# First batch of an attention + expert kernel: packed x rows, weights loaded and converted up front, the weights' product beside the first block

## The chip, the cores and the metric

The kernel runs on one core of one Trainium2 chip. The metric is the device time of one execution in microseconds (us), as the median of several runs. All arithmetic is on the chip; the host only lays the inputs out anew.

## The reference

`x` is 4 batches of 12480 rows of 128 numbers, `inducing` is 32 rows of 128. A first attention lets the 32 inducing rows look at all rows of a batch and gives 32 pooled rows `h`; a second lets every row of `x` look at the 32 pooled rows. Each output row then goes through an expert layer of width 2048 with a rational activation.

```
def mab(q, kv):
    s = scale * (q @ kv.transpose(0, 2, 1));  s = s - s.max(-1, keepdims=True)
    a = np.exp(s);  a /= a.sum(-1, keepdims=True) + 1e-09
    return a @ kv
h = mab(I, x);  y = mab(x, h)

h = y @ w_in                                   # 128 -> 2048
P = a[0] + a[1]*h + a[2]*h**2 + a[3]*h**3
Q = 1 + |b[0]|*|h| + |b[1]|*h**2
out = (P / (Q + 1e-6)) @ w_out                 # 2048 -> 128
```

The weights `w_in` and `w_out` arrive as 64-bit floats, shown to the kernel as 64-bit integers.

## The kernel before, in words

A batch is cut into 26 blocks of 480 rows (`BT`). Groups of four blocks (seven groups, `NG`) share the attention steps. The kernel has three parts.

**Boot (`before`)** serves batch 0 alone. `pass1(0)` loads x by columns (`wide_columns`, 960 KB a group), multiplies by the inducing rows on PE, and DVE copies the scores into `e` with their maxima; ACT takes the exponentials (`exp_rows`). `pooled(0)` turns `e` on PE (`turned`, `pt`), ACT copies it to `eT`, and PE multiplies it with x by rows (`wide_rows`, three blocks to a tile) into `ph`, which DVE adds up in `acc`. A column of ones behind each x row (the 129th) gives the sum of the weights. `fold`, a reciprocal and a product give the pooled rows `HT`. All these x tiles live in the nine slots of one big tile called `row`, taken in turn. The 11 weight pieces (`raw`, five of `w_in`, six of `w_out`) are loaded in the middle of this; `convert_weights` makes 32-bit floats of each with three DVE TENSOR_SCALAR, three DVE SCALAR_TENSOR_TENSOR and one POOL addition between the last two of them. `Params` loads the six numbers a and b and `derive` works some 90 tiny DVE operations on them. In `before` the instructions are not pinned to program order; a scheduler orders them.

**Start of the main part (`main`)**: in program order from here on. Block group 0 goes through `pass3` (scores against `HT`: `pd`, `sT`, `ps`, `a`, turned back: `pa`, split into `hl`, spread by 16 small DMAs into `at`). Then two of four `piece`s fold `HT` into `w_in` (`pg`, `gs`, `st`), `shift_parts` builds `by` and `same` on POOL, and `w_out` is scaled on DVE.

**The units**: 832 units, eight for each of the 104 blocks. A unit is `first` (PE, `hp`), for every second unit a further product with `by`, `same` into `hp` (`moved`); a mask on DVE or an absolute value on ACT; a DVE product into `l`; logarithms and sigmoids of ten units at a time on ACT, over several slots of `row`; a last product on DVE and POOL; and, 17 units after `first`, `second` (PE, `po`). Engines run in order. A block's last unit also needs `lin`, made by `linear` from `w_two` and `base`; for batch 0 these come from `products` (the sum over `w_out` on DVE, 16 turns of `w_in`, 32 products `pl`). Between the units `side` lets two generators go on as a plan of spare time allows: `attend` (later groups' `pass3`) and `ahead` (first `products`, `linear(0)`, `bounded(0)`, then `pass1`, `pooled` and the pieces of the next batch). While `linear` of batch 0 is not ready, only `ahead` goes on:

```
for which in ("attend", "ahead") if not self.fast or "linear" in self.ready_cols[0] else ("ahead",):
```

PSUM tiles in boot and at the start of main come from a ring of three (`misc`, tag `hp`).

Of the kernel before, what the change touches and what calls it, by code (L numbers as in the profile page):

```python
# [9 lines left out]
F32 = mybir.dt.float32  # L10
# [25 lines left out]
def convert_weights(nc, t, raw, dst, width):  # L36

    words = raw.bitcast(I32).rearrange("p (f two) -> p f two", two=2)
    lo, hi = words[:, :, 0], words[:, :, 1]
    a, b, c = (t[:, width * i:width * i + width].bitcast(I32) for i in range(3))  # L40
# [6 lines left out]
    V.tensor_scalar(out=c, in0=hi, scalar1=0x7FF00000, scalar2=None, op0=ALU.bitwise_and)  # L47
    nc.gpsimd.tensor_tensor(out=bf, in0=bf, in1=af, op=ALU.add)
    V.scalar_tensor_tensor(out=dst, in0=c, scalar=float(0x38100000), in1=bf, op0=ALU.is_ge, op1=ALU.mult)

# [141 lines left out]
class Kernel:  # L192
# [37 lines left out]
    def misc(self, name):  # L230
        self.holder = self.who
        if self.boot:
            return self.ps_h.tile([P, 2, 512], F32, tag="hp", name=name)[:, 0]
        return self.ps_m.tile([P, 512], F32, tag="misc", name=name)

    def free(self):
        self.holder = None

    def cast(self, engine, out, in_):
# [106 lines left out]
    def wide_columns(self, b):  # L346
# [8 lines left out]

        ts = [load(g) for g in range(min(4, self.NG))]
        for g in range(self.NG):
            if g + 4 < self.NG:
                ts.append(load(g + 4))
            t = ts.pop(0)  # L360
            for j in range(4):
                yield t[:, BT * j:BT * j + BT]
                if j == 0 and g > 0:
                    self.wide_rows(b)

    def wide_rows(self, b):

        xs = self.xs.setdefault(b, [])
        n = min(3 * HB, self.NCH - HB * len(xs))
        if n > 0:  # L370
            t = self.room(f"xw{b}_{len(xs)}")[0:TP, 0:n * (C + 1)].rearrange("p (c d) -> p c d", d=C + 1)
            self.nc.sync.dma_start(out=t[:, :, 0:C], in_=self.x_t[b, :, HB * len(xs):HB * len(xs) + n, :])
            self.nc.gpsimd.memset(t[:, :, C:], 1.0)
            xs += [t[:, HB * i:HB * i + HB] for i in range(n // HB)]
# [71 lines left out]
    def pooled(self, b, own=None):  # L446
# [16 lines left out]

        eTs, early = [], int(self.boot)
        while self.e_done.get(b, 0) < self.NG:
            self.flush()
            yield "wait", 0
        if early:
            yield from turned(0)
        for g in range(self.NG):  # L470
            nb = min(4, self.NB - 4 * g)
# [5 lines left out]
            for k in range(HB * nb):  # L477
# [8 lines left out]
                nc.tensor.matmul(ph[M * c:M * c + M, 0:C + 1], eT[:, c, M * j:M * j + M], xs[4 * g + j][:, c, :], start=(j == 0), stop=(j == nb - 1))  # L486
                if c == HB - 1 and not self.boot and 4 * g + j + 4 < self.NB:
                    xs.append(self.x_rows(b, 4 * g + j + 4))
            yield "v", 0.2
            if g == 0:  # L490
                nc.vector.tensor_copy(out=acc, in_=ph[:, 0:C + 1])
            else:
                nc.vector.tensor_tensor(out=acc, in0=ph[:, 0:C + 1], in1=acc, op=ALU.add)
            self.free()
# [59 lines left out]
    def split(self, b, which, st, g):  # L554
# [10 lines left out]
        self.ready_cols[b].add(which)  # L565

    def products(self):


        nc, cp, ap, p = self.nc, self.cp, self.ap, self.params  # L570
        self.w_two = cp.tile([C, C], F32, name="w_two")
        self.base = cp.tile([P, C], F32, name="base")
        both = ap.tile([P, 512], F32, tag="gs", name="both", bufs=2)
        level, w_sum = both[:, 0:P], both[:, P:P + C]
        nc.gpsimd.tensor_scalar(out=level, in0=self.ident, scalar1=0.0, scalar2=p.lin_shift, op0=ALU.mult, op1=ALU.add)
        for i in range(2):
            yield "v", 1.2
            c = slice(C // 2 * i, C // 2 * (i + 1))
            nc.vector.tensor_reduce(out=w_sum[:, c], in_=self.w_out[:, :, c].rearrange("p f d -> p d f"), axis=mybir.AxisListType.X, op=ALU.add)
        yield "pe", 0.25  # L580
# [40 lines left out]
    def thirds(self, b, g):  # L621
# [16 lines left out]
        V.memset(lin[rest, C:], 0.0)  # L638

    def bounded(self, b):  # L640

        nc, ap, p = self.nc, self.ap, self.params
        if b == 0:
            for j in range(4):
                for i, op in ((j, ALU.max), (4 + j, ALU.min)):
                    yield "v", 0.6
                    nc.vector.tensor_reduce(out=self.w_max[:, i:i + 1], in_=self.w_in[:, 512 * j:512 * j + 512], axis=mybir.AxisListType.X, op=op)
            yield "v", 0.3
            nc.vector.scalar_tensor_tensor(out=self.w_max[:, 0:4], in0=self.w_max[:, 4:8], scalar=-1.0, in1=self.w_max[:, 0:4], op0=ALU.mult, op1=ALU.max)
            nc.vector.tensor_reduce(out=self.w_max[:, 4:5], in_=self.w_max[:, 0:4], axis=mybir.AxisListType.X, op=ALU.max)  # L650
        yield "v", 0.15
# [123 lines left out]
    def ahead(self):  # L775

        if self.fast:
            yield from self.products()
            yield from self.linear(0)
            yield from self.bounded(0)  # L780
        for b in range(1, self.B):
            self.cols[b, "a"] = self.columns(b, "a")
            yield "wait", 0
            yield "wait", 0
            yield from self.pass1(b)
            yield from self.pooled(b)
            while self.left < b - 2:
# [249 lines left out]
    def before(self):  # L1037

        nc = self.nc
        self.e, self.xs, self.HT, self.issued, self.tick = {}, {}, {}, {}, 0  # L1040
        self.boot, self.direct, self.holder, self.who = True, True, None, None
# [3 lines left out]
        loads, words = self.weights(), []  # L1045
        for n, _ in enumerate(self.pass1(0)):
            if n >= 18 and n % 3 == 1:
                words += [w for w in [next(loads, None)] if w]
        self.params = Params(self.tc.nc, self.cp, self.moe_a, self.moe_b)
        for n, _ in enumerate(self.pooled(0, self.cp.tile([C, 4 * M], F32, name="HT0"))):  # L1050
            if n % 8 == 5:
                words += [w for w in [next(loads, None)] if w]
        words += list(loads)
# [3 lines left out]
        for n, (raw, dst, width) in enumerate(words):  # L1057
            convert_weights(nc, self.room(f"cv{n}"), raw, dst, width)

# [21 lines left out]
    def main(self, fast):  # L1081
# [4 lines left out]
        self.act_q, self.jobs, self.gens, self.need = [], [], {}, {}  # L1086
        self.tick, self.ended, self.boot, self.holder, self.left = 0, 0, True, None, -1
        self.splits, self.spreads, self.scored, self.fetched, self.sent = 0, 0, -1, False, (0, 0)
        self.direct = True
# [22 lines left out]
    def again(self):  # L1112

        for n, (raw, dst, width) in enumerate(self.weights()):
            convert_weights(self.nc, self.room(f"cva{n}"), raw, dst, width)
        self.main(False)
# [58 lines left out]
```

## Time and profile before

| | |
|---|---|
| median of 3 runs | 2311.43 us (2310.86 to 2311.54) |
| the profiled execution: its time, its span | 2313.14 us, 2311.3 us |
| PE, DVE, ACT, POOL busy | 2146.0, 2147.9, 2101.0, 1483.0 us |
| first copy of an output block (`oT`), second, last | 182.97, 215.60, 2304.47 us |

Busy times are shares of an engine's instructions in the span; matmul ends are modelled. The three busiest engines lie close together, so a stage has to be looked at by itself. A wait in brackets is the idle time before an instruction and what ended it.

### The profile page before, as it was taken

Reading aid. Unit: us, or ns where it says so; the run is one execution under the profiler, and the core shown is the slowest. Engines: PE = TensorE matmul, PEld = TensorE weight load, DVE = VectorE, ACT = ScalarE, POOL = GpSimd, SP = SyncE. Lnnn points to the kernel's source line nnn. Section 1 sums busy time; section 2 is a strip of 40 time slices with the busy share of each in tenths; the row PEclk is TensorE's granted clock in tenths of the full one; section 3 lists DMA queues with packets and bytes.
Section 4 is the critical chain, followed back from the end, with each engine's and each line's share of the span. In section 5 each row is a group of like instructions: output and inputs, shape, how many; then the busy total and the mean of one; then the engine's idle time right before and its main releaser. Section 6 shows DMA issues by size and latency. Waiting matters only on the chain.

```text
span 2311.3 us, 23789 instructions
## 1 busy us (share of the span) xinstructions
PE 2146.0 (93%) x7744; PEld 975.0 (42%) x7744; DVE 2147.9 (93%) x2368; ACT 2101.0 (91%) x1193; POOL 1483.0 (64%) x1039
## 2 busy tenths in 40 slices
PE   5377999999899999998999999989999999999997
PEld 2133444444344444443444444434444444444443
DVE  2788999999999999999999999999999999999994
ACT  1086999999899999998999999989999999999995
POOL 0334666676666666766666676766677676766666
PEclk6588999999999999999999999999999999999999
DMA  9302220131123101311231031001101000000000
GB/s 242 96 1 86 83 80 21 48 81 44 47 90 91 58 25 50 74 60 46 76 93 55 18 87 43 26 16 54 52 22 50 23 18 31 18 19 20 18 17 15
DMA packets 117103, 120.89 MB, mean 52 GB/s; under 512 B 13289, under 2 KB 115561, under 8 KB 116969
## 3 DMA queue, kind: packets, MB, share of 16 engines
q1 hardware_dynamic: 116969, 119.28, 17.9%
q8 instruction: 63, 1.03, 0.2%
q14 instruction: 71, 0.58, 0.1%
HBM read 80.89 MB, written 25.56 MB: 46 GB/s over the span
## 4 chain that ended last, share of the span: by engine, by line
PE 47%; DVE 20%; ACT 16%; issue 12%; POOL 2%; DMA 2%; SPq 1%; DVEq 0%; POOLq 0%; ACTq 0%
PE po L176 31%; ACT row L176 13%; PE hp L176 12%; DVE l L176 10%; DVE row L176 6%; ACT L176 2%; SPq L176 1%; PE ph L176 1%; DMA row<-x_c 1%; POOL l L176 1%; PE pd L176 1%; PE pc L176 1%; POOL row L176 1%; DVE gl L176 1%; DVE oT L176 1%
## 5 line engine op out<-in xcount | busy, mean ns | idle before, releaser
L176 PE MATMUL po<-l,w_out 128*128 128x480 f32 x3328 | 1563.5, 575 | 6.1 <-POOL l L176 3.4
L176 DVE SCALAR_TENSOR_TENSOR l<-row,all,hp 128x960 f32<-128x960 f32 x832 | 999.5, 1202 | 32.4 <-ACT row L176 23.7
L176 POOL TENSOR_TENSOR l<-row 128x960 f32<-128x960 f32 x416 | 929.2, 2234 | 34.7
L176 POOL TENSOR_SCALAR row<-l,all 128x960 f32<-128x960 f32 x416 | 448.1, 1077 | 673.8 <-DVE l L176 603.8
L176 PEld LDWEIGHTS po<-l,w_out 128*128 128x128 f32 x3328 | 619.4, 191 | 405.8 <-issue 239.6
L176 ACT ACTIVATE row<-row,all 128x3840 f32<-128x3840 f32 (+1 forms) x250 | 738.1, 2953 | 1.0
L176 ACT ACTIVATE row<-row 128x3840 f32<-128x3840 f32 (+1 forms) x250 | 715.9, 2864 | 8.0 <-DVE l L176 6.8
L176 DVE SCALAR_TENSOR_TENSOR l<-l,all,row 128x960 f32<-128x960 f32 x416 | 533.3, 1283 | 4.6 <-ACT row L176 4.6
L176 PE MATMUL hp<-at,st 128*128 128x480 f16 x1664 | 477.2, 369 | 42.8 <-DVE l L176 32.9
L176 ACT ACTIVATE row<-hp,all 128x960 f32<-128x960 f32 x416 | 436.7, 1050 | 62.2 <-PE hp L176 61.3
L176 DVE TENSOR_SCALAR row<-hp 128x960 int32<-128x960 int32 x416 | 475.4, 1143 | 11.4 <-PE hp L176 10.7
L176 PEld LDWEIGHTS <-st 128*128 128x128 f16 x1872 | 181.9, 98 | 527.0 <-issue 506.8
L176 PE MATMUL hp<-same,by 96*128 96x480 f16 x832 | 239.6, 369 | 31.2 <-DVE row L176 24.6
L176 ACT ACT_TABLE_LOAD x169 | 216.8, 1283 | 3.5 <-PEq L1168 0.7
L176 PEld LDWEIGHTS <-by 96*128 96x128 f16 x832 | 82.0, 99 | 222.5 <-issue 195.6
L176 DVE COPY oT<-po 128x480 f32<-128x480 f32 x104 | 67.6, 650 | 46.5 <-PE po L176 45.6
L176 PE MATMUL po<-at,st 128*128 128x480 f16 x208 | 60.0, 370 | 3.2 <-DVE st L176 3.2
L176 ACT ACTIVATE a<-a 120x512 f32<-120x512 f32 (+2 forms) x21 | 14.7, 723 | 37.0 <-DVE a L176 37.0
L176 ACT ACTIVATE e<-e,nmc 128x960 f32<-128x960 f32 (+1 forms) x16 | 15.5, 984 | 31.5 <-DVE nmc L176 31.5
L176 DVE TENSOR_SCALAR_CACHE_REDUCE e<-pc 128x240 f32<-128x240 f32 (+1 forms) x56 | 20.6, 397 | 24.4 <-PE pc L176 24.4
L176 POOL TENSOR_TENSOR a<-a,asm 120x512 f32<-120x512 f32 (+1 forms) x27 | 38.7, 1433 | 1.7 <-PE bound L176 1.7
L176 POOL TENSOR_TENSOR row<-row 128x384 f32<-128x384 f32 (+2 forms) x11 | 11.9, 1085 | 42.8 <-DVE row L176 35.3
(117 smaller groups left out, 595.4 us busy)
## 6 DMA issues: line engine op xcount, KB each, us to landing
xTb<-x_c SPq DMA_DIRECT2D x104, 240.0 KB, 3.2
out<-oT SPq DMA_DIRECT2D x104, 240.0 KB, 2.0
xTa<-x_c SPq DMA_DIRECT2D x78, 240.0 KB, 3.3
x<-x_t SPq DMA_DIRECT2D x78, 240.0 KB, 4.0
at<-hl SPq DMA_DIRECT2D x416, 30.0 KB, 1.8
row<-x_t SPq DMA_DIRECT2D x8, 720.0 KB, 14.1
row<-x_c SPq DMA_DIRECT2D x5, 960.0 KB, 11.7
raw<-w_in SPq DMA_DIRECT2D x4, 480.0 KB, 12.0
```

The costliest lines, as they stand in the source:

```text
L176: ins = call(*args, **kw)
```

## The change

Seven edits, all in what is done for batch 0 or around its first blocks.

1. x rows for batch 0 are stored without the column of ones (slots of 128 instead of 129 floats); the sums of the weights come from DVE reductions over `e`, `n` is 128 in boot.
2. The parameters are loaded and derived first, `shift_parts` follows them; both stood later. `before` is now in program order.
3. The five `w_in` pieces are asked for ahead of x; all seven column loads are issued at once; a `w_out` piece is asked for before each row load from the third on.
4. `converted` emits the conversions between the steps of `pass1` (five) and `pooled` (six), the last operation of one behind the front of the next, in tiles of their own. Masked words overwrite `lo`.
5. `sums`: `w_out` is scaled on POOL (it was DVE), `base`'s level made, and `w_out` summed on DVE in two halves, inside `pooled`.
6. In `main` the two pieces and `products` are stepped between the steps of `pass3` of group 0, instead of behind it and among the units.
7. The maxima of `w_in` and `bounded(0)` go behind `pass1(1)`.

```
     def wide_rows(self, b):
...
+            if len(xs) >= 2 * 3:
+                self.words += [w for w in [next(self.loads, None)] if w]
-            t = self.room(f"xw{b}_{len(xs)}")[0:TP, 0:n * (C + 1)].rearrange("p (c d) -> p c d", d=C + 1)
-            self.nc.sync.dma_start(out=t[:, :, 0:C], in_=self.x_t[b, :, HB * len(xs):HB * len(xs) + n, :])
-            self.nc.gpsimd.memset(t[:, :, C:], 1.0)
+            t = self.room(f"xw{b}_{len(xs)}")[0:TP, 0:n * C].rearrange("p (c d) -> p c d", d=C)
+            self.nc.sync.dma_start(out=t, in_=self.x_t[b, :, HB * len(xs):HB * len(xs) + n, :])

+    def converted(self, words):
+        last = ()
+        for n, (raw, dst, width) in enumerate(words):
+            t = self.mp.tile([P, 2, width], I32, tag="l", name=f"cv{n}", bufs=self.rooms["l"])
+            gen = convert_weights(self.nc, t, raw, dst, width)
+            next(gen)
+            for _ in last:
+                pass
+            last = gen
+            yield
...
     def pooled(self, b, own=None):
...
+            full, rest = self.NB // 4, self.NB % 4
+            nc.vector.tensor_reduce(out=acc[:, C:], in_=e[:, 0:full].rearrange("p g n -> p (g n)"), ...)
...
+    def sums(self):
...
+        nc.gpsimd.tensor_scalar(out=self.w_out, in0=self.w_out, scalar1=p.z_rho, scalar2=None, op0=ALU.mult)
+        nc.gpsimd.tensor_scalar(out=self.base, in0=self.ident, scalar1=0.0, scalar2=p.lin_shift, ...)
+        for i in range(2):
+            yield
+            c = slice(C // 2 * i, C // 2 * (i + 1))
+            nc.vector.tensor_reduce(out=self.w_two[:, c], in_=self.w_out[:, :, c].rearrange("p f d -> p d f"), ...)
...
     def before(self):
...
+        nc.state["pin"] = True
+        self.params = Params(self.tc.nc, self.cp, self.moe_a, self.moe_b)
         self.setup()
+        self.loads, self.words = self.weights(), []
+        first = [next(self.loads) for _ in range(-(-self.F // BT))]
+        ahead = self.pass1(0)
+        next(ahead)
         self.params.derive()
+        self.shift_parts()
...
+        more = self.converted(first)
+        next(more)
+        next(more)
+        for n, _ in enumerate(ahead):
+            if n % 4 == 3:
+                next(more, None)
+        self.drive(more)
+        more = self.later_words()
+        for n, _ in enumerate(self.pooled(0, ...)):
+            if n > 8 and n % 3:
+                next(more, None)
+        self.drive(more)
+
+    def later_words(self):
+        yield from self.converted(self.words)
+        yield from self.sums()
...
     def main(self, fast):
...
-        self.drive(self.pass3(0, [range(1)]))
-        for piece in pieces[:2]:
-            self.drive(piece)
+        fill = pieces[:2] + ([self.products()] if fast else [])
+        while_held = 0
+        for _ in self.pass3(0, [range(1)]):
+            held, while_held = self.held, while_held + 1 if self.held else 0
+            while fill and while_held < 3:
+                if next(fill[0], self) is self:
+                    fill.pop(0)
+                if self.held == held:
+                    break
+        for gen in fill:
+            self.drive(gen)
         self.later = pieces[2:]
-        if fast:
-            self.shift_parts()
-            nc.vector.tensor_scalar(out=self.w_out, in0=self.w_out, scalar1=p.z_rho, scalar2=None, op0=ALU.mult)
```

`self.held` counts the PSUM tiles that `misc` has given and `free` has not had back. `next(fill[0])` is called until that count is what it was.

## Rows read from the trace of the kernel before

**Rows 1.** Busy time of each engine by stage, then clock, DMA share, GB/s.

```profile
core 0: us, PE busy (x) PEld busy (x) DVE busy (x) ACT busy (x) POOL busy (x), PEclk, DMA share, GB/s
0.00:37.70 37.70, 17.11 (x67) 3.95 (x70) 6.94 (x38) 5.51 (x7) 1.56 (x15) 0.71 1.00 255
...
70.00:94.50 24.50, 5.31 (x10) 1.22 (x10) 22.29 (x53) 0.00 (x0) 9.51 (x9) 0.57 0.27 83
94.50:106.20 11.70, 5.53 (x13) 2.60 (x14) 5.69 (x9) 4.06 (x8) 1.15 (x1) 0.57 0.05 13
106.20:131.40 25.20, 13.43 (x38) 5.27 (x39) 17.29 (x16) 8.00 (x11) 9.21 (x20) 0.73 0.05 14
131.40:215.60 84.20, 62.83 (x213) 29.55 (x213) 65.83 (x83) 66.31 (x41) 30.97 (x21) 0.84 0.13 41
338.25:2304.50 1966.25, 1904.19 (x6743) 868.04 (x6742) 1889.73 (x1909) 1896.61 (x1059) 1347.49 (x916) 0.99 0.15 44
```

**Rows 2.** Timeline of batch 0's chain, from the exponentials to the first unit.

```profile
33.47 3.65 ACT L176 ACTIVATE e<-e,nmc 128x960 f32<-128x960 f32 x4 [31.45 <-DVE nmc L176]
...
70.93 0.29 DVE L176 COPY HT<-HT 128x128 f32<-128x128 f32 x1 [0.24 <-PE HT L176]
...
94.49 0.66 DVE L176 COPY sT<-pd 128x480 f32<-128x480 f32 x1 [0.44 <-DVE w_out L176]
...
100.42 1.06 PE L176 MATMUL pa<-ident,a 120*128 120x120 f32 x4 [4.11 <-DVE a L176]
...
106.18 0.98 PE L176 MATMUL hp<-at,st 128*128 128x480 f16 x4 [1.35 <-POOL st L176]
```

**Rows 3.** Timeline of the first units: waits for `by`, the sum, `linear`.

```profile
112.94 0.98 PE L176 MATMUL hp<-same,by 96*128 96x480 f16 x2 [5.77 <-POOL by L176]
...
118.77 3.70 DVE L176 TENSOR_REDUCE both<-w_out 128x64 f32<-128x1024 f32 x2
...
180.32 1.06 PE L176 MATMUL po<-at,st 128*128 128x480 f16 x2 [3.19 <-DVE st L176]
```

**Rows 4.** ACT from 106 to 216 us: a wait, and a group of instructions.

```profile
ACT row L176 <- PE hp L176: 11.2, 2, 8.5
...
L176 ACT ACTIVATE wt<-pgt,all 128x512 f32<-128x512 f32 x4 | 2.7, 686 | 0.0
```

**Rows 5.** Windows of the load stream: columns of x, rows of x, `derive`.

```profile
8.00:17.00 9.00, 6.06 (x28) 0.74 (x28) 2.99 (x17) 0.00 (x0) 0.48 (x4) 0.94 1.01 423
20.00:30.00 10.00, 3.25 (x12) 0.45 (x12) 1.11 (x8) 0.00 (x0) 0.12 (x1) 0.50 1.11 186
56.00:66.00 10.00, 1.85 (x32) 1.09 (x24) 9.51 (x96) 0.59 (x2) 1.19 (x1) 0.50 1.02 224
```

**Rows 6.** DMA of the first 75 us: packets by size; an issue's time to landing.

```profile
DMA packets 17779, 18.01 MB, mean 240 GB/s; under 512 B 948, under 2 KB 16368, under 8 KB 17776
...
ind<-ind_c SPq DMA_DIRECT2D x1, 16.0 KB, 1.6
```

**Rows 7.** Timeline of two conversions of `w_out` pieces, from 81 us.

```profile
81.43 0.35 DVE L176 TENSOR_SCALAR row<-raw 128x384 int32<-128x384 int32 x1
...
82.64 1.15 DVE L176 TENSOR_SCALAR row<-raw 128x384 int32<-128x384 int32 x1
83.70 0.55 DVE L176 SCALAR_TENSOR_TENSOR w_out<-row 128x384 f32<-128x384 int32 x1
...
86.72 0.55 DVE L176 SCALAR_TENSOR_TENSOR w_out<-row 128x384 f32<-128x384 int32 x1
```

**Rows 8.** The page's costliest groups: a POOL TENSOR_SCALAR.

```profile
L176 POOL TENSOR_SCALAR row<-l,all 128x960 f32<-128x960 f32 x416 | 448.1, 1077 | 673.8 <-DVE l L176 603.8
```

**Rows 9.** PE's four turns and two chains of products, at either clock.

```profile
126.58 1.06 PE L176 MATMUL pgt<-ident,w_in 128*128 128x128 f32 x4
...
131.94 1.05 PE L176 MATMUL pl<-w_out,wt 128*128 128x128 f32 x8
...
142.35 2.08 PE L176 MATMUL pl<-w_out,wt 128*128 128x128 f32 x8 [0.46 <-ACT wt L176]
```

**Rows 10.** Instructions on tile `w_max`, durations min, median, max in ns.

```profile
L176 DVE TENSOR_REDUCE w_max<-w_in x8: 669/674/677, 183.5 to 201.6; 128x1 f32<-128x512 f32 x8
```

More of the change, by code (lines that the diff above doesn't have):

```diff
@@ L39, in convert_weights @@
     lo, hi = words[:, :, 0], words[:, :, 1]
-    a, b, c = (t[:, width * i:width * i + width].bitcast(I32) for i in range(3))
+    a, b = t[:, 0], t[:, 1]
     V = nc.vector
@@ L231, in misc @@
         self.holder = self.who
+        self.held += 1
         if self.boot:
@@ L237, in free @@
         self.holder = None
+        self.held -= 1
     def cast(self, engine, out, in_):
@@ L317, in weights @@
             yield raw, dst, width
+    def converted(self, words):
[8 more added lines that the diff above has]
+            yield
+        for _ in last:
+            pass
+        yield
     def x_rows(self, b, n):
@@ L354, in load @@
             return t
[L356 to L360, printed above, removed]
+        ts = [load(g) for g in range(self.NG)]
+        for g, t in enumerate(ts):
             for j in range(4):
@@ L462, in turned @@
             eTs.append(eT)
-        eTs, early = [], int(self.boot)
+        eTs, early, n = [], int(self.boot), C if self.boot else C + 1
         while self.e_done.get(b, 0) < self.NG:
@@ L469, in pooled @@
             yield from turned(0)
+            full, rest = self.NB // 4, self.NB % 4
+            nc.vector.tensor_reduce(out=acc[:, C:], in_=e[:, 0:full].rearrange("p g n -> p (g n)"), axis=mybir.AxisListType.X, op=ALU.add)
+            if rest:
+                more, rows = ap.tile([P, 1], F32, tag="mx", name=f"sum{b}"), slice(0, M * rest)
+                nc.vector.tensor_reduce(out=more[rows], in_=e[rows, full], axis=mybir.AxisListType.X, op=ALU.add)
+                nc.vector.tensor_tensor(out=acc[rows, C:], in0=acc[rows, C:], in1=more[rows], op=ALU.add)
         for g in range(self.NG):
@@ L485, in pooled @@
                     self.wide_rows(b)
[L486 removed]
+                nc.tensor.matmul(ph[M * c:M * c + M, 0:n], eT[:, c, M * j:M * j + M], xs[4 * g + j][:, c, :], start=(j == 0), stop=(j == nb - 1))
                 if c == HB - 1 and not self.boot and 4 * g + j + 4 < self.NB:
@@ L490, in pooled @@
             if g == 0:
-                nc.vector.tensor_copy(out=acc, in_=ph[:, 0:C + 1])
+                nc.vector.tensor_copy(out=acc[:, 0:n], in_=ph[:, 0:n])
             else:
-                nc.vector.tensor_tensor(out=acc, in0=ph[:, 0:C + 1], in1=acc, op=ALU.add)
+                nc.vector.tensor_tensor(out=acc[:, 0:n], in0=ph[:, 0:n], in1=acc[:, 0:n], op=ALU.add)
             self.free()
@@ L565, in split @@
         self.ready_cols[b].add(which)
-    def products(self):
[L570 to L579, printed above, removed]
+    def sums(self):
+        nc, p = self.nc, self.params
+        self.w_two = self.cp.tile([C, C], F32, name="w_two")
+        self.base = self.cp.tile([P, C], F32, name="base")
+        nc.gpsimd.tensor_scalar(out=self.w_out, in0=self.w_out, scalar1=p.z_rho, scalar2=None, op0=ALU.mult)
+        nc.gpsimd.tensor_scalar(out=self.base, in0=self.ident, scalar1=0.0, scalar2=p.lin_shift, op0=ALU.mult, op1=ALU.add)
+        for i in range(2):
+            yield
+            c = slice(C // 2 * i, C // 2 * (i + 1))
+            nc.vector.tensor_reduce(out=self.w_two[:, c], in_=self.w_out[:, :, c].rearrange("p f d -> p d f"), axis=mybir.AxisListType.X, op=ALU.add)
+    def products(self):
+        nc, ap, p = self.nc, self.ap, self.params
+        level, w_sum = self.base, self.w_two
         yield "pe", 0.25
@@ L638, in thirds, with magnitudes @@
         V.memset(lin[rest, C:], 0.0)
+    def magnitudes(self):
+        nc = self.nc
+        for j in range(4):
+            for i, op in ((j, ALU.max), (4 + j, ALU.min)):
+                yield "v", 0.6
+                nc.vector.tensor_reduce(out=self.w_max[:, i:i + 1], in_=self.w_in[:, 512 * j:512 * j + 512], axis=mybir.AxisListType.X, op=op)
+        yield "v", 0.3
+        nc.vector.scalar_tensor_tensor(out=self.w_max[:, 0:4], in0=self.w_max[:, 4:8], scalar=-1.0, in1=self.w_max[:, 0:4], op0=ALU.mult, op1=ALU.max)
+        nc.vector.tensor_reduce(out=self.w_max[:, 4:5], in_=self.w_max[:, 0:4], axis=mybir.AxisListType.X, op=ALU.max)
     def bounded(self, b):
         nc, ap, p = self.nc, self.ap, self.params
[L643 to L650, printed above, removed]
         yield "v", 0.15
@@ L785, in ahead @@
             yield from self.pass1(b)
+            if self.fast and b == 1:
+                yield from self.magnitudes()
+                yield from self.bounded(0)
             yield from self.pooled(b)
@@ L1087, in main @@
         self.tick, self.ended, self.boot, self.holder, self.left = 0, 0, True, None, -1
+        self.held = 0
         self.splits, self.spreads, self.scored, self.fetched, self.sent = 0, 0, -1, False, (0, 0)
@@ L1112, in again @@
     def again(self):
-        for n, (raw, dst, width) in enumerate(self.weights()):
-            convert_weights(self.nc, self.room(f"cva{n}"), raw, dst, width)
+        self.drive(self.converted(self.weights()))
         self.main(False)
```

20 lines of the change are left out of this document (4 added, 16 removed).

## The prediction

> **What bounds the kernel now.** I read the busy time by stage first. From 338 us to the end, ACT is busy 1897, PE 1904 and DVE 1890 of 1966 us [rows 1]: nothing in the change touches these units, and a gain must come from before. The early stages look otherwise. Up to 37.7 us DVE works 6.9 us; from 70 to 94.5 us it works 22.3 of 24.5 while ACT does nothing; from 131.4 to 215.6 us, where the units already run and logarithms and sigmoids are on, ACT is busy only 66.3 of 84.2 us [rows 1].
>
> The timeline then says what is late. `HT` of batch 0 is ready at 71.2, but the copy `sT` that uses it starts at 94.49: DVE, in order, converts weights in between [rows 2]. From `sT` the chain runs through `pa` at 100.42 to the first unit's product at 106.18 [rows 2]. That unit waits 5.8 us for POOL's `by`; DVE sums `w_out` for 3.7 us at 118.8 with the units' work behind it; and block 0's last product waits for `linear` until 180.3, since `products` had to squeeze between the units [rows 3]. ACT's 17.9 us of idleness after 131.4 hold 11.2 us in two waits for PE's `hp`, which stands behind that product [rows 4]; the rest is group 1, which `attend` may start only once `linear` is there.
>
> The load stream: with column loads alone 423 GB/s, while the row loads dominate 186 [rows 5]. The packet counts say why: 16368 of 17779 packets are under 2 KB, and the rows of x (6.39 MB in pieces of 512 bytes, 12480 of them) are most of these [rows 6]. A tile of 129 floats a row cannot take two rows in one run, one of 128 can.
>
> **The change part by part.**
>
> *Loads.* 2.1 MB of `w_in`, 6.4 of columns, 6.4 of rows and 2.1 of `w_out` are 17 MB. At 423 for the whole [rows 5], less a bit for the 1 KB runs of `w_out`, they take some 42 to 45 us after a start at 3 us: the last at 47 or so. If the rows stay at 186, they alone take 34 us instead of 15 and the last comes at about 65. I take the fast end: the columns' runs are the nearest to the new ones. `w_in` in front moves the columns by 5 us (2.1 MB at 423), but the rows no longer sit between them, so the last group lands at about 24 us.
>
> The Trainium skill, "DMA: Bandwidth & Descriptors", Specifications, puts the least transfer for line rate at 512 B, which the rows of x already are. By that sentence packing them would bring the stream nothing; the windows, 186 against 423 GB/s, speak against it [rows 5]. By it the sum below would end near 2287 instead of 2282.
>
> *DVE to the exponentials.* The parameters land first, some 3 us after issue (a lone small load took 1.6 [rows 6]), so `derive` starts near 4 and takes about 7 (its window holds 9.5 us with a piece of a conversion in it [rows 5]). Five conversions follow among the score copies. One `w_out` conversion took 3.0 us, from 83.70 to 86.72, of which 0.8 is a TENSOR_SCALAR of 1.15 us that takes 0.35 when POOL is not adding [rows 7]. Four at 3.0 and a small one at 1.2 are 13.2; 2 more for the first addition, which queues behind `shift_parts` on POOL; 6.9 for everything DVE did in this stage before [rows 1]; 2 for the trips to PE in the chain of maxima. 4 + 7 + 13.2 + 2 + 6.9 + 2 = 35 us for the start of the exponentials (33.47 before [rows 2]): the conversions are hidden in what was DVE's wait for columns. If that cover fails, each costs its 3 us.
>
> *DVE to `sT`.* Exponentials 3.7 us [rows 2], to 38.7. The new sum over `e`, 3360 elements: at 0.674 us for 512 [rows 10], 4.4, to 43. Six `w_out` conversions, 5 x 3.0 + 1.2 = 16.2, to 59.3; they stand in front of the second group's `acc`, so PE waits, its ring of three PSUM tiles full. POOL's scaling of `w_out`, 2048 columns at 1.077 us for 960 [rows 8], 2.3 us, during which DVE has nothing: 61.6. The two sums, 3.7 [rows 3]: 65.3. The groups held back need about 6, the fold and `HT` 3.4, and `pd` 2: `sT` at 76.7, **17.8 us earlier**. Bounds: 68 with conversions at 2.2 and no such waits, 88 if the words land late and nothing overlaps. The eight POOL memsets and DVE's scaling vanish, but hid behind waits: nothing.
>
> *`sT` to the first unit.* It was 11.7 us [rows 2]. Now two pieces, the base and four rounds of turns, copy and products stand in PE's queue ahead of `pa`. A round is 1.06 + 0.69 + 2.08 at the low clock and about 0.6 + 0.69 + 1.05 at the high one [rows 4, 9], plus hand-overs: 4.0 or 2.5 us, and the rounds don't overlap, as each `pl` waits for ACT's copy with the next turns behind it. The granted clock here was 0.57 [rows 1], so I lean to the low: 15 us, in place of the 4.1 that PE waited for DVE anyway. The `pg` in front of `ps` add 2. What the later pieces and `st` cost after `pa` was hidden by the small DMAs and saves nothing. I take **12 us more** (bounds 8 and 16): the first unit at 106.2 - 17.8 + 12 = 100.4, **5.8 us earlier**.
>
> *First units to 131.4.* The wait for `by` (5.8) and the sum on DVE (3.7) are gone [rows 3], the turns and `base` on PE as well (about 1): **10 us** (bounds 6 and 12).
>
> *131.4 to 215.6.* ACT loses four copies, 2.7 us [rows 4], and has 17.9 us of idle time to lose [rows 1]: 20.6 at most. `linear` is ready in the first ticks, `attend` and `ahead` start some 20 units earlier. But their DVE work then falls on the filling units; I take **16 us** (bounds 8 and 20.6).
>
> *Moved back.* The eight maxima of `w_in`, 8 x 0.67 = 5.4 us [rows 10], go from here to the preparation of batch 1, where DVE is 96% busy: **3 us lost** (bounds 0 and 5.4). The slots of `row` start at another number, which shifts the pattern of joined logarithms; it runs through all nine positions either way: nothing, at most a microsecond or two at the end.
>
> Sum: 5.8 + 10 + 16 - 3 = 28.8 us. The profiled execution took 2313.1 with a span of 2311.3; the median is 2311.4, so the same gain from it gives 2282.6, and I say **2282**. Ends with all bounds together: best 8.7 earlier at `sT` more and 4 less on the way, 2 + 4.6 + 3, or 51 us of gain (2260); worst -11.3, -4, -4, -8, -2.4, or 1 us of loss.
>
> **The rivals.**
>
> *The boot gives nothing.* DVE's order makes the start no earlier: the first unit comes at about 106, because the chain with `products` in it costs 16 and `sT` comes only at 84 to 85. For it: DVE idles during the maxima's trips, the exponentials and POOL's scaling, and in order nothing fills that. Then only the later 23 us remain: about 2288 to 2293.
>
> *The rows stay slow.* Packing changes no rate: behind the columns at 24, seven row tiles at 186 GB/s take 27 us and the `w_out` pieces among them 5 or more, so the last word lands near 58 and its conversion ends near 64 instead of 59: 5 us, 2287. The page of the Trainium skill named above would have it so; the two windows are the evidence against.
>
> *Given back.* The later units don't keep the lead: earlier work of `attend` and `ahead` lands on a full DVE, and the known stalls at the batches' ends take it, 10 to 20 us: 2292 to 2302. For it: three engines within 1% of each other [rows 1]. Against: ACT's idle time in this stage is real, and work done early isn't done twice.
>
> *All of it and more.* High clock, rounds at 2.5 us, ACT full: 2262.
>
> *Slower.* One mechanism: the last `w_out` conversions stand in DVE's queue ahead of the sums that `HT` needs, and their loads now stand behind row loads, which wait in SP's queue for slots that PE must have read. If that stream crawls, `HT` and all behind it wait. The gain behind the first unit is 23 us, so it decides when the first unit comes after 129, which by the steps above is a last word at about 47 + 29 = 76 us, 17 MB at about 230 GB/s. At 186 throughout, the last word lands at 94: about 2329. Rows 5 show 423 for long runs, so this is unlikely.
>
> **How the numbers follow.** Forecast 0.55 (2270 to 2288 is its own range), boot gives nothing 0.14, rows slow 0.08, given back 0.09, more 0.07, slower 0.05, no change 0.02. Range: 2264 to 2302 leaves out about half of "more", the slow end, and the edges of the costs not seen. Under 0.2% (4.6 us) a measurement of this kernel tells nothing. Faster by more: 0.91; within: 0.04, of which 0.02 is the end of "given back"; slower: 0.05.
>
> **What would show it.** Row loads above 350 GB/s and the last load before 50 us; exponentials at 33 to 37 us; `sT` near 77 with the `w_out` conversions ahead of `acc`; `pa` some 18 us behind `sT`, with PE's `pl` and ACT's `wt` in turn between; the first unit near 100; no wait for `by`; the first output copy 30 us earlier than 183; ACT idle under 5 us from the first logarithms to the second output copy. The prediction fails if `sT` comes after 88, if the rounds cost over 4 us each, or if the lead at the second output copy shrinks by the end by more than 10 us.

## The result, and the profile after

The changed kernel takes 2289.83 us (median of 4 runs, 2288.05 to 2293.07); the kernel before, run beside it, 2311.48 (2310.86 to 2311.94). The ratio is 0.9908, 95% interval 0.9891 to 0.9925: 21.65 us faster, 7.8 us above the forecast of 2282. That is within the range 2264 to 2302, but just outside the forecast's own 2270 to 2288 and inside the 2288 to 2293 of the rival "the boot gives nothing". The profiled execution took 2290.83 us with a span of 2288.9.

Four marks cut the gain of the profiled execution into stages: `sT`, the first unit's product, the second output copy, the last one. All numbers are us.

| stage | before | after | gain | forecast |
|---|---|---|---|---|
| to `sT` | 94.49 | 82.93 | 11.6 | 17.8 |
| `sT` to the first unit | 11.69 | 21.84 | -10.1 | -12 |
| first unit to second copy | 109.42 | 85.95 | 23.5 | 26 |
| second copy to last | 2088.87 | 2091.39 | -2.5 | -3 |
| sum | | | 22.4 | 28.8 |

Nearly all of the gain lies in the third row; the gain up to `sT` is spent again on the way to the first unit. These are lines of the timeline after (start, duration, engine, line, instruction; in brackets the wait and its releaser):

```profile
36.62 3.65 ACT L177 ACTIVATE e<-e,nmc 128x960 f32<-128x960 f32 x4 [30.55 <-DVE nmc L177]
...
39.73 3.15 DVE L177 TENSOR_REDUCE acc<-e 128x1 f32<-128x2880 f32 x1 [3.14 <-ACT e L177]
...
45.78 1.15 DVE L177 TENSOR_SCALAR cv<-raw 128x384 int32<-128x384 int32 x1
...
50.30 0.34 DVE L177 TENSOR_SCALAR cv<-raw 128x384 int32<-128x384 int32 x1
50.68 0.56 DVE L177 SCALAR_TENSOR_TENSOR cv<-raw,cv 128x384 int32<-128x384 int32 x1
51.27 0.36 DVE L177 TENSOR_SCALAR cv<-cv 128x384 int32<-128x384 int32 x1
...
58.86 0.36 DVE L177 TENSOR_SCALAR cv<-raw 128x384 int32<-128x384 int32 x1 [1.46 <-DMA raw<-w_out]
...
60.95 1.10 POOL L177 TENSOR_TENSOR cv<-cv 128x384 f32<-128x384 f32 x1 [3.96 <-DVE cv L177]
...
61.11 1.35 DVE L177 SCALAR_TENSOR_TENSOR w_out<-raw,cv 128x384 f32<-128x384 int32 x1
...
62.64 0.23 DVE L177 TENSOR_SCALAR cv<-raw 128x128 int32<-128x128 int32 x1 [0.18 <-DMA raw<-w_out]
...
65.08 5.46 POOL L177 TENSOR_SCALAR w_out<-w_out,all 128x2048 f32<-128x2048 f32 x1 [0.72 <-DVE w_out L177]
...
70.57 3.64 DVE L177 TENSOR_REDUCE w_two<-w_out 128x64 f32<-128x1024 f32 x2 [5.40 <-POOL w_out L177]
...
82.93 0.66 DVE L177 COPY sT<-pd 128x480 f32<-128x480 f32 x1 [2.04 <-PE pd L177]
...
90.06 2.08 PE L177 MATMUL pl<-w_out,wt 128*128 128x128 f32 x8 [0.84 <-ACT wt L177]
...
93.83 1.16 PE L177 MATMUL pl<-w_out,wt 128*128 128x128 f32 x8 [0.84 <-ACT wt L177]
...
99.69 0.58 PE L177 MATMUL pa<-ident,a 120*128 120x120 f32 x4
...
104.77 1.76 PE L177 MATMUL hp<-at,st 128*128 128x480 f16 x4 [4.51 <-DMA at<-hl]
106.98 0.96 PE L177 MATMUL hp<-same,by 96*128 96x480 f16 x2 [0.45 <-DVE row L177]
...
169.18 0.66 DVE L177 COPY oT<-po 128x480 f32<-128x480 f32 x1 [0.56 <-PE po L177]
...
190.72 0.66 DVE L177 COPY oT<-po 128x480 f32<-128x480 f32 x1
...
2282.11 0.66 DVE L177 COPY oT<-po 128x480 f32<-128x480 f32 x1 [11.13 <-PE po L177]
```

`sT`, `pa` and `hp` answer to [rows 2]. No conversion stands between `HT` and `sT` any more; the conversions now stand ahead of `HT`, and POOL's scaling of `w_out` makes DVE wait 5.40 us. The `pl` and `wt` of the product stand between `sT` and `pa`, and `hp` waits 4.51 us for the small DMAs. The wait for `by` of [rows 3] is gone.

The windows (busy time of PE, PEld, DVE, ACT, POOL, clock, DMA share, GB/s) answer to [rows 1] and [rows 5]:

```profile
18.00:26.00 8.00, 4.40 (x24) 0.46 (x16) 7.79 (x20) 0.00 (x0) 1.98 (x2) 0.51 1.03 383
26.00:31.00 5.00, 2.01 (x12) 0.44 (x10) 4.83 (x14) 0.00 (x0) 1.42 (x1) 0.50 1.01 225
...
46.00:51.00 5.00, 1.87 (x39) 1.22 (x36) 4.83 (x9) 0.60 (x1) 1.88 (x2) 1.00 0.99 212
51.00:56.00 5.00, 1.18 (x25) 0.64 (x24) 4.76 (x10) 0.60 (x1) 1.35 (x2) 0.63 1.03 215
...
120.00:190.72 70.72, 60.26 (x210) 23.21 (x210) 65.39 (x78) 64.57 (x37) 30.96 (x20) 0.85 0.30 90
```

In the first four, DVE works nearly all the time, where it had been mostly idle (1.11 of 10 us from 20 to 30 us in [rows 5]). The row loads, from 26 us on, run at 212 to 225 GB/s, not at the columns' rate. In the last, ACT is busy 64.57 of 70.72 us.

### The profile page after: what moved, and what is told of

Read it like the earlier page. It is cut to its first block, busy times and chain, and to the rows that moved or that the text cites. A ratio compares the mean times of both kernels' runs of the same rounds, so it can differ in the third digit from the quotient of the medians.

```text
span 2288.9 us, 23773 instructions
## 1 busy us (share of the span) xinstructions
PE 2141.9 (94%) x7744; PEld 969.5 (42%) x7744; DVE 2154.6 (94%) x2370; ACT 2101.7 (92%) x1193; POOL 1489.4 (65%) x1031
## 3 DMA queue, kind: packets, MB, share of 16 engines
q8 instruction: 63, 1.03, 0.2%
## 4 chain that ended last, share of the span: by engine, by line
PE 41%; DVE 27%; issue 14%; ACT 12%; DMA 3%; POOL 1%; SPq 1%; DVEq 0%; ACTq 0%; POOLq 0%
PE po L177 26%; DVE l L177 15%; PE hp L177 10%; ACT row L177 10%; DVE row L177 7%; DMA raw<-w_out 2%; ACT L177 1%; SPq L177 1%; PE ph L177 1%; PE pd L177 1%; DVE oT L177 1%; PE pc L177 1%; POOL l L177 1%; PE pg L177 1%; DVE asm L177 1%
## 5 line engine op out<-in xcount | busy, mean ns | idle before, releaser
L177 ACT ACTIVATE eT<-pt 120x512 f32<-120x512 f32 (+1 forms) x28 | 15.5, 558 | 31.6 <-PE pt L177 31.6
L177 POOL TENSOR_TENSOR cv<-cv 128x384 f32<-128x384 f32 (+2 forms) x11 | 12.3, 1119 | 37.3 <-DVE cv L177 37.2
L177 PE MATMUL pt<-ident,e 128*120 128x128 f32 (+1 forms) x112 | 18.3, 293 | 17.8 <-DVE acc L177 16.4
## 6 DMA issues: line engine op xcount, KB each, us to landing
row<-x_t SPq DMA_DIRECT2D x8, 720.0 KB, 21.8
row<-x_c SPq DMA_DIRECT2D x5, 960.0 KB, 11.6
```

Of the source, the lines that this page charges most:

```text
L177: ins = call(*args, **kw)
```

## The experiments

Ratios are to the kernel before, run beside each experiment (medians 2311.97 to 2312.36). Times of single instructions come from one profiled execution each, and these differ: ahead of `sT` numbers 4, 6, 7 and 12 leave the changed kernel as it is, yet their `sT` comes at 79.96, 83.10, 81.42 and 81.63 us (82.93 in the changed kernel). DVE's waits for weight words there add up to anything from 0 (number 4) to 2.84 us (number 6), and PE's steps behind them ran at either clock (granted 0.50 from 80 to 84 us in the changed kernel, 1.00 in numbers 7 and 12). So a shift of 3 us or less at `sT` shows little unless the wait or the instruction that makes it is seen too.

**1. Rows of x over 128 partitions.** The tiles of the changed kernel cover 120; here the DMA brings eight rows more, which nobody reads.

```
-            t = ...[0:TP, 0:n * C].rearrange("p (c d) -> p c d", d=C)
-            self.nc.sync.dma_start(out=t, in_=self.x_t[b, :, HB * len(xs):HB * len(xs) + n, :])
+            t = ...[:, 0:n * C].rearrange("p (c d) -> p c d", d=C)
+            flat = self.x_t.rearrange("b p n c -> (b p) n c")[TP * b:TP * b + P]
+            self.nc.sync.dma_start(out=t, in_=flat[:, HB * len(xs):HB * len(xs) + n, :])
+            t = t[0:TP]
```

> The changed kernel with its nine row loads over 128 partitions (eight rows of the next batch more, never read) instead of 120. Theory A: the rows' rate is set by the 120 partitions, not by the length of their runs; then the row stretch moves at 380 GB/s or more where the changed kernel shows 212 to 225, and the last weight piece lands near 47 us instead of 62. DVE is full with conversions from 43 to 65 us there and waits only 1.6 us for loads, so the first unit comes only 2 to 4 us earlier and the time is 2286 to 2289. Theory B: what holds the rate is the stream itself (row loads and weight loads mixed, or many loads in flight): 215 GB/s stays and so does the time, 2290.

2291.42 us (2289.26 to 2296.16), ratio 0.9914 [0.9894, 0.9935]. The windows of this kernel:

```profile
26.00:31.00 5.00, 2.02 (x12) 0.45 (x10) 4.80 (x14) 0.00 (x0) 1.41 (x1) 0.50 1.03 401
...
36.00:41.00 5.00, 2.54 (x10) 2.05 (x10) 1.20 (x2) 4.15 (x6) 0.00 (x0) 0.50 1.03 390
...
46.00:51.00 5.00, 1.41 (x35) 1.14 (x36) 4.83 (x10) 0.49 (x1) 2.12 (x2) 1.00 0.75 290
51.00:56.00 5.00, 2.26 (x35) 1.47 (x33) 4.77 (x9) 0.60 (x1) 1.17 (x1) 0.52 0.01 3
```

With 128 partitions the same rows come at about 400 GB/s and the stream ends near 50 us, as the forecast had it. In both kernels the 16 DMA engines are busy all the time on average (share 1.01 to 1.03 from 26 to 31 us), so the packets themselves take longer. Between 27 and 46 us a 6 KB packet of the rows took 446 ns (median of the trace's DMA records) with 120 partitions and 239 with 128; a 1 KB packet of `w_out`, whose loads cover 128 partitions in both, 78 and 46 ns. The slow rows thus slow their neighbours too. Yet `sT` moves by 1.6 us only (81.35), the first unit by 1.4 (103.40), where 2 to 4 were expected, and the time not measurably: DVE was full with conversions, and only its waits for words, 1.64 us, are gone.

**2. Rows not packed.** Slots of 129 floats again, the rest as changed.

```
-            t = ...[0:TP, 0:n * C].rearrange("p (c d) -> p c d", d=C)
+            t = ...[0:TP, 0:n * (C + 1)].rearrange("p (c d) -> p c d", d=C + 1)[:, :, 0:C]
```

> The changed kernel with the row slots 129 floats apart again (512-byte runs), and nothing else; the column of ones is not written and not read. Theory A (partitions): the row stretch loses at most a tenth of its rate, 190 to 205 GB/s, last weight piece 3 to 5 us later, time 2290 to 2294. The prediction's reading (run length sets the rate) would have the two alike only if packing brought nothing; if packing matters at all beyond a tenth, the time rises by over 5 us, to 2295 or more.

2294.6 us (2292.19 to 2297.77), 0.9923 [0.9905, 0.994]. Its windows:

```profile
26.00:31.00 5.00, 2.01 (x12) 0.44 (x10) 4.81 (x14) 0.00 (x0) 1.42 (x1) 0.50 1.15 187
...
46.00:51.00 5.00, 2.02 (x38) 1.52 (x37) 4.83 (x9) 0.60 (x1) 2.02 (x2) 0.84 1.14 193
```

`sT` (86.40) and the first unit (108.46) come 3.5 and 3.7 us later. In the six windows from 26 to 56 us the rate is 175 to 197 GB/s; packing is worth 19 to 40 GB/s, window by window, about a seventh. The time's interval overlaps that of the changed kernel, so what packing is worth in time is not shown.

**3. `w_out` scaled on DVE again.** (`nc.gpsimd.tensor_scalar` becomes `nc.vector.tensor_scalar` in `sums`.)

> The changed kernel with w_out scaled by DVE, at the same place, instead of by POOL. POOL's instruction took 5.46 us with DVE idle for 5.4 of them; on DVE it took 1.28 us in the kernel before. If a gain in the boot is handed on whole to the end, the copy sT comes 4.2 us earlier, at 78.7, and the time is 2285 to 2286. Rival: the units' filling or the load on DVE takes it back: 2289 or more.

2286.23 us (2283.71 to 2290.06), 0.9889 [0.9869, 0.9909]. Its timeline:

```profile
65.37 1.29 DVE L177 TENSOR_SCALAR w_out<-w_out,all 128x2048 f32<-128x2048 f32 x1
66.77 3.73 DVE L177 TENSOR_REDUCE w_two<-w_out 128x64 f32<-128x1024 f32 x2
...
78.07 0.66 DVE L177 COPY sT<-pd 128x480 f32<-128x480 f32 x1 [1.56 <-PE pd L177]
```

From the end of the last conversion to the sums DVE takes 1.4 us, not 5.6. `sT` comes 4.9 us earlier than after the change, the first unit 6.7 earlier (98.08). The medians differ by 3.6 us, less than their intervals can tell apart.

**4. The product of the weights among the units**, as before; all else as changed.

```
-        fill = pieces[:2] + ([self.products()] if fast else [])
+        fill = pieces[:2]
...
     def ahead(self):
...
+            yield from self.products()
             yield from self.linear(0)
```

> The changed kernel with products (the base, four rounds) back where it was: first thing that ahead does among the units; the pieces stay stepped into the block's chain. Theory: the gain behind the first unit comes from linear being ready in the first ticks. Then the first unit comes 8 to 9 us earlier (pa no longer behind the rounds), near 96, but the wait for linear in block 0 and the late start of attend are back (10 and 12 us in the kernel before): second output copy near 200 to 205 instead of 190.7, time 2298 to 2303. Rival: the rounds fit into the idle time of the filling units and only the earlier first unit counts: 2281 to 2284.

2302.3 us (2300.93 to 2303.63), 0.9958 [0.9946, 0.997]. Its timeline:

```profile
93.64 1.76 PE L177 MATMUL hp<-at,st 128*128 128x480 f16 x4 [4.51 <-DMA at<-hl]
...
159.38 0.65 DVE L177 COPY oT<-po 128x480 f32<-128x480 f32 x1
...
201.87 0.66 DVE L177 COPY oT<-po 128x480 f32<-128x480 f32 x1 [0.95 <-PE po L177]
```

The first unit comes 11.1 us earlier than after the change (3.0 of them already at `sT`, where nothing was changed, so the rounds cost some 8) and the first copy 9.8, but the second copy 11.2 us later, the last 10.1; the median is 12.5 us higher. An early `linear`, which sets `attend` free, is worth more than an early first unit.

**5. In the kernel before, `shift_parts` alone moved early** (behind `derive`).

> The kernel before with one part of the change alone: shift_parts (by and same on POOL) right behind derive instead of behind the first pieces. Theory: the 5.8 us that the first unit waited for by are taken off the path one for one, since all units stand behind that wait: 2305 to 2307 where the kernel before has 2311 to 2312. Rival: the wait for linear 70 us later is set by products, not by the first unit, and takes it back: 2310 to 2312.

2306.36 us (2303.32 to 2307.53), 0.9975 [0.9965, 0.9985]. Its timeline:

```profile
107.93 1.78 PE L176 MATMUL hp<-at,st 128*128 128x480 f16 x4 [1.27 <-POOL st L176]
110.16 0.96 PE L176 MATMUL hp<-same,by 96*128 96x480 f16 x2 [0.45 <-DVE row L176]
```

The 5.77 us of [rows 3] become 0.45; the first unit starts 1.7 us later, the second copy 3.7 earlier, the last 5.8 earlier, and the median falls by 6.0. Within the noise, this wait was worth its full length.

**6. Maxima and `bounded(0)` early again**, right behind `linear(0)`.

```
             yield from self.linear(0)
+            yield from self.magnitudes()
+            yield from self.bounded(0)
...
             yield from self.pass1(b)
-            if self.fast and b == 1:
-                yield from self.magnitudes()
-                yield from self.bounded(0)
```

> The changed kernel with the maxima of w_in and bounded(0) back behind linear(0), so 5.4 us of DVE among the filling units instead of in the preparation of batch 1. The prediction's step (moving them back costs 3 us) would have it up to 3 us faster, 2285 to 2289. Rival: DVE is the fuller engine among the filling units too, and the maxima cost their 5 us there: 2293 to 2296.

2279.13 us (2277.73 to 2280.18), 0.9854 [0.984, 0.9869]: 10.7 us under the changed kernel, where at most 3 were expected. First the timeline of the changed kernel, then that of this one: `HT` of batch 1 and, for this one, the second and the last copy.

```profile
565.71 0.28 DVE L177 COPY HT<-HT 128x128 f32<-128x128 f32 x1
```

```profile
191.79 0.66 DVE L177 COPY oT<-po 128x480 f32<-128x480 f32 x1
...
508.03 0.27 DVE L177 COPY HT<-HT 128x128 f32<-128x128 f32 x1
...
2271.20 0.66 DVE L177 COPY oT<-po 128x480 f32<-128x480 f32 x1 [11.12 <-PE po L177]
```

The second copy is 1.07 us later than in the changed kernel, the rest 12.0 us shorter (2079.41 for 2091.39). In the changed kernel the maxima run from 270.7 to 381.4 us; `pass1(1)`, 70 us earlier than before (maximum of its scores at 270.65, was 341.06), hands its lead to them, and `HT` of batch 1 comes at 565.71, where it was 560.76 before. With the maxima early it comes 58 us sooner.

Most of the 12.0 us lies in one stretch: the 41st to the 46th output copy take 113.5 us after the change and 103.1 here. Number 4 has 103.1 in it too, with the maxima where the change put them; its `HT` of batch 1 came at 522.60 and that of batch 2 at 972.18. These are `HT` of batch 2 in the changed kernel, in this one, and in number 12:

```profile
1021.61 0.27 DVE L177 COPY HT<-HT 128x128 f32<-128x128 f32 x1
...
956.23 0.27 DVE L177 COPY HT<-HT 128x128 f32<-128x128 f32 x1
...
1027.79 0.27 DVE L177 COPY HT<-HT 128x128 f32<-128x128 f32 x1
```

In number 12 `HT` of batch 1 comes earlier still (490.54), but that of batch 2 late, and the stretch takes 110.1 us. So in these runs the stretch is short where batch 2 is prepared early, not where batch 1 is. Number 4 has nothing of it at the end, as it was 7.7 us behind by the 41st copy, counted from the second. Why the early preparation shortens the stretch is not shown.

**7. The fill stops after 13 steps of `pass3`**, so that `pa` does not stand behind all rounds (`while fill and while_held < 3 and k < 13`).

> The changed kernel with only two of the four rounds of products stepped in ahead of pa; the other two stand behind the block's small DMAs. If the rounds are what delays pa (2.4 to 3.5 us each), pa comes at 94 to 95 instead of 99.7 and the first unit's product at 99.5 to 100.5 instead of 104.8, since the two late rounds fit into the 4.5 us that PE waited for the DMA; time 2285 to 2286. Rival: the late rounds end behind the landing and hold the first unit, which gains under 2 us: 2288 to 2290.

2288.73 us (2286.08 to 2292.47), 0.9906 [0.9889, 0.9923]: no change that can be told. `pa` starts at 91.59 (8.1 us earlier, 1.5 of them already at `sT`) and the first unit no longer waits for the small DMAs, but comes at 99.49 only; the second copy is 5.5 us earlier, the last 4.8 in the profiled execution, which was the fastest of the four.

**8. Edits 1, 3 and 7 together, and two `w_out` conversions ahead of the sum over `e`** (`if n < 2 or n > 8 and n % 3`).

> The changed kernel with row loads over 128 partitions, w_out scaled on DVE, two of the four rounds of products behind the block's DMAs, and the first two w_out conversions issued before the sum over e, where DVE waited 3.1 us for the exponentials. Theory: the steps add up in front of the first unit (1.4, 5, 5 and 3 us): sT at 73 to 76, first unit at 90 to 93, time 2277 to 2281. Rival: with the words there in time the filling units become the bound and hand on half: 2283 to 2286.

2280.52 us (2278.56 to 2282.82), 0.9865 [0.985, 0.9881]. `sT` at 75.27, first unit 92.28, second copy 177.78, last 2269.89. The lead over the changed kernel is 12.9 us at the second copy and 12.2 at the end.

**9. Edits 8 and 6 together.**

> The four edits of the run before that joined them (rows over 128 partitions, w_out scaled on DVE, two rounds of products behind the block's DMAs, two conversions ahead of the sum), and also the maxima and bounded(0) back behind linear(0). Theory: the first is worth 9 us ahead of the first unit and the second 10 us at the batches' preparation, at different places, so they add: 2268 to 2272. Rival: both move the preparation of the later batches in time and the second gain belongs to one position only: 2276 to 2281.

2265.15 us (2264.72 to 2269.17, five runs), 0.9803 [0.979, 0.9816]. Its timeline:

```profile
155.67 0.66 DVE L177 COPY oT<-po 128x480 f32<-128x480 f32 x1
...
177.21 0.66 DVE L177 COPY oT<-po 128x480 f32<-128x480 f32 x1
...
493.46 0.27 DVE L177 COPY HT<-HT 128x128 f32<-128x128 f32 x1
...
2255.95 0.66 DVE L177 COPY oT<-po 128x480 f32<-128x480 f32 x1 [11.13 <-PE po L177]
```

This beats both kernels, the changed one by 24.7 us. The two edits do not get in each other's way: number 8 by itself gave 9.3 us, number 6 gave 10.7. Together they gave 4.7 more than that sum, and 3 more than expected; where this comes from is not shown.

**10. POOL's scaling with a second operation** (`scalar2=0.0, op1=ALU.add`, which adds zero).

> The changed kernel with POOL's scaling of w_out written as multiply by the scalar and add 0 (two operations) instead of multiply alone. If the form is what made 2048 columns take 5.46 us where a two-operation instruction of this kernel takes 1.07 us for 960, it takes 2.3 us. Rival: something else about the place or the operand (16 x 128, in place): 5.4 us again.

One run, 2286.55 us. All instructions on `w_out`, POOL's line (duration in ns, least, median, most; first and last start):

```profile
L177 POOL TENSOR_SCALAR w_out<-w_out,all x1: 1972/1972/1972, 64.9 to 64.9; 128x2048 f32<-128x2048 f32 x1
```

1.97 us in place of 5.46. DVE waits 1.91 us for it, not 5.40. `sT` comes at 79.39 and the first unit at 101.01, 3.5 and 3.8 us earlier.

**11. Each row load in two DMAs, of 112 and of 8 partitions.**

```
-            self.nc.sync.dma_start(out=t, in_=self.x_t[b, :, HB * len(xs):HB * len(xs) + n, :])
+            for r in (slice(0, 112), slice(112, TP)):
+                self.nc.sync.dma_start(out=t[r], in_=self.x_t[b, r, HB * len(xs):HB * len(xs) + n, :])
```

> The changed kernel with each row load cut in two: partitions 0 to 111 and 112 to 119. If what slows the rows is that 120 partitions are no multiple of 16, the large part moves at the rate of the columns and the stretch at 330 GB/s or more. Rival: only all 128 (or a multiple of 32 or 64) reach it: 230 GB/s or less again.

One run, 2291.35 us. Its windows:

```profile
26.00:31.00 5.00, 2.01 (x12) 0.44 (x10) 4.83 (x14) 0.00 (x0) 1.42 (x1) 0.50 1.02 225
...
46.00:51.00 5.00, 3.19 (x38) 2.08 (x36) 4.79 (x10) 0.60 (x1) 1.57 (x2) 0.50 1.06 224
```

217 to 225 GB/s from 26 to 56 us, as with 120 partitions in one DMA.

**12. Maxima and `bounded(0)` later still**, behind `linear(1)`.

> The changed kernel with the maxima and bounded(0) moved further back: behind linear(1), when batch 1 is prepared, instead of between pass1(1) and pooled(1). The same work in the same batch. Theory: what they cost is that ahead stands still for them from 270 to 384 us, so that HT of batch 1 comes at 566 instead of 508 us; then HT(1) comes near 500 to 515 here, the stretch to block 35 is 4 to 6 us faster than in the changed kernel, and the end 2281 to 2287, as batch 2 is delayed instead. Rival: it is the 5.4 us of DVE in the preparation, wherever: 2289 to 2292.

2283.3 us (2279.4 to 2285.66), 0.9879 [0.9864, 0.9894], 6.5 us under the changed kernel. From second copy to last 2084.36 us: 7.0 less than after the change, 5.0 more than in number 6. `HT` of batch 1 comes at 490.54. So more than half of the price hung on the place ahead of that `HT`, and the rest is still paid in the later place. `HT` came earlier than the 500 to 515 expected and earlier than in number 6, so its time alone does not set the price.

This profiled execution shows one thing more. Nothing is changed ahead of the units, yet the timeline has the product's rounds at another clock:

```profile
86.93 1.16 PE L177 MATMUL pl<-w_out,wt 128*128 128x128 f32 x8 [0.84 <-ACT wt L177]
89.36 1.16 PE L177 MATMUL pl<-w_out,wt 128*128 128x128 f32 x8 [0.84 <-ACT wt L177]
...
100.31 1.76 PE L177 MATMUL hp<-at,st 128*128 128x480 f16 x4 [4.51 <-DMA at<-hl]
```

The first `pl` takes 1.16 us, not 2.08, and the first unit stands 18.7 us behind `sT` (81.63) in place of 21.8. From 80 to 84 us the granted clock was 1.00 here (2.4 GHz) and 0.50 after the change (1.2 GHz). In the 4 us ahead of that PE had been busy 2.70 us in both, and the clock was 0.68 on average here, 0.50 there. Why one execution got it earlier is not shown.

## Why the prediction came out as it did

**The mechanism was right behind the first unit, and the boot's was not.** The larger part of the forecast gain came as forecast: no wait for `by`, no sum over `w_out` among the units, `linear` early (`gl` of batch 0 at 113.91, was 176.13). First unit to second copy gave 23.5 us for 26; the ACT time left idle there from 120 us on is 6.2 us, a little over the 5 that were named. Numbers 4 and 5 show the two parts by themselves: 12.5 us for the product's place (net of the 8 us that the rounds cost ahead of the first unit), 6.0 for `by`. One sign failed: the first output copy came 13.8 us earlier, not 30.

**The step "Loads" failed.** It took the rate from the length of the runs. The packets did become fewer (6387 for 17779 in the first 75 us), but the row loads went from 186 GB/s to no more than 212 to 225, and DVE first got at the last `w_out` words at 62.6 us. This is the mechanism of the rival "rows stay slow", at a smaller price: 1.6 us of waits where the rival had 5. Numbers 1 and 2 part the causes: 128 partitions in place of 120 bring the 400, packing about a seventh. The columns of [rows 5] differ from the rows in both, and the forecast saw only the one. The Trainium skill, "DMA: Bandwidth & Descriptors", Specifications, whose 512 B the forecast set aside, was the nearer to what packing did: 19 to 40 GB/s, where the forecast had over 200.

**DVE to `sT`: two terms sized low.** The exponentials came at 36.62 (forecast 35) and the sum over `e` took 3.15 and 0.63 us for 4.4, so both the forecast and the trace begin the conversions at 43 to 43.6. They end at 65.0, not 59.3. Loads account for about 1.6 us of this: DVE waited 1.46 and 0.18 us for words. Number 1, without these waits, has `sT` 1.6 us earlier, at the same clock. Most of the rest is DVE's own time: a conversion came every 3.5 us, not 3.0. The operation beside POOL's addition is not the difference, as it is 0.8 us longer in both kernels: a TENSOR_SCALAR before ([rows 7]), the last operation after, 1.35 us for 0.55. The 0.5 us lie in the four steps between a conversion's first five operations. There each operation reads what the one before wrote, or overwrites what it read, and starts 0.03 to 0.04 us after that one's end (50.30 + 0.34, then 50.68); before, the next one started 0.08 us ahead of the end (84.17 + 0.35, then 84.44), as two conversions' operations stood mixed. The forecast took 3.0 us from the old order. POOL's scaling was the mis-sized term: 5.46 us for 2.3, as the price per column of a POOL instruction with two operations [rows 8] was put on one with a single operation. Numbers 3 and 10 show it: between the last conversion and the sums it was worth 4.2 and 3.5 us. What follows the sums was shorter, 8.7 us for 11.4, so `sT` missed by 6.2 us: 5.7 and 3.2 late, 2.7 back.

**`sT` to the first unit** came out at +10.1 us for +12, but not by the low clock throughout. Only the first round cost 3.8 us; the others cost 2.43, the forecast's price at the high clock, and the four took 11 us, not 15. Against this stands the way from `sT` to the first turns, 5.7 us, where the forecast's figures leave some 3.8. So this number is near in part because two errors meet. Number 12 shows that the same instructions can also get the high clock; the forecast had that only as part of "all of it and more".

**"Moved back" was mis-sized, and an unforeseen gain covered it.** The maxima were costed as DVE time, 3 us. Their place cost 10.7 us (number 6), and 15.4 behind another start (between numbers 8 and 9). Numbers 6 and 12 point to what waits behind them in `ahead`, the preparation of batches 1 and 2. With the maxima early, the part from the second copy on is 9.5 us shorter than in the kernel before (2088.87 to 2079.41). That `attend` and `ahead` start earlier would explain this gain, but no run shows it by itself. So -2.5 for a forecast of -3 is luck: two errors that meet. Block intervals of 23 us or more are still in the trace, at blocks 12, 23, 34, 43, 44, 65 and 66 after the change; with the maxima early there are fewer, at 20, 40, 41 and 62. How each of them follows from a late `HT` is not shown.

**"The boot gives nothing"**, at a chance of 0.14, describes the result better than the forecast's own sum: the first unit came at 104.77, 1.4 us earlier (5.8 forecast, about 106 in the rival), and the time lies in the rival's range. Its two reasons do not give its 106 (`sT` at 84 to 85 and 16 us more than before would be 112); what came was `sT` at 82.93 and 10.1 more. Number 8, with the first unit at 92.28, shows that more was there to be had.

## What to carry to other kernels

Before a load's rate is forecast from the length of its runs, compare the partitions as well: the loads that ran fast and slow here differed in both. Work that is moved in the program has to be priced by what stands behind it in its own generator or queue, not only by its own microseconds. A cost read from one order of instructions need not hold in another: the conversion went from 3.0 to 3.5 us when its operations stood one behind the other. When a stage is shortened, look for the thing that sets another stage free (here `linear`), as its place counts more than when the first unit starts.

## What the runs showed of the hardware that was not expected

- **Partitions.** Loads of 6 KB runs over 120 partitions moved 212 to 225 GB/s, over 128 partitions 390 to 404, with nothing else changed but eight rows more. Splitting off eight partitions did not help (217 to 225). The Trainium skill, "DMA: Bandwidth & Descriptors", in the part on how many engines a DMA uses ("Why a DMA increments its semaphore by 16 and not by 1"), would give a DMA over 120 partitions 15 of 16 engines, by our estimate a loss of a sixteenth, and one over 112 all 16; the runs do not fit that. The Trainium skill, "SBUF — State Buffer", Door 1, has the rate go by the ports that the partitions reach, and by its table 120 reach all 16; the runs do not fit that either. The advice of the same page of the Trainium skill, in the section "The DMA setup-cost knee", to use 128 partitions holds, for more than either rule gives (about 218 against 400 GB/s). What halves the rate stays open.
- **POOL.** A TENSOR_SCALAR with one operation on 128x2048 floats took 5.46 us, with two operations 1.97, on DVE 1.29.
- **POOL and DVE.** The conversion's last operation on DVE, with two inputs in SBUF, took 1.35 us beside a POOL addition of 1.10. The Trainium skill, "SBUF — State Buffer", Who interferes with whom, says that such an instruction contends with a POOL instruction that reads SBUF, and the trace agrees. A TENSOR_SCALAR with one input was held as well: 1.15 us beside the addition, 0.35 alone.
